# Sliding-window attention with an MLP mixer behind it: half tails on all 128 columns, the last product by blocks of tokens, and another order from the third batch on

## The chip, the cores and the metric

The kernel runs on one core of a Trainium2 chip. The metric is the time of one execution on the device in microseconds (us). An execution is about 280 us long, so 0.2% of it is 0.56 us.

The engines are named as the profile names them: PE is TensorE's matmul, PEld its weight load, DVE is VectorE, ACT is ScalarE, POOL is GpSimd and SP is SyncE, which here only issues DMAs. Results of PE land in PSUM, which has eight banks of 128 partitions by 512 float32.

## The reference

Inputs are q, k, v of 8 batches x 8 heads x 576 tokens x 64, and four weight matrices.

```python
scores = q @ k.T / sqrt(64) - slope[h] * abs(rel)      # rel = query - key
attn   = softmax(where((rel >= 0) & (rel < 128), scores, -1e9))
x      = (attn @ v), heads side by side                # 8 x 576 x 512
h      = relu(x.T @ w_tok1) @ w_tok2                   # mixes tokens, 576 -> 256 -> 576
u      = x + h.T
out    = u + relu(u @ w_ch1) @ w_ch2                   # mixes channels, 512 -> 1536 -> 512
```

## The kernel before, in words

**Tiles.** The batches go in pairs. The 576 tokens of a batch are four blocks of 128 and a tail of 64; the two tails of a pair share one block of 128 rows, the pair's ninth block (`TAIL`). The window is 128, so a block of queries sees its own keys and those of the block before.

**Attention, per block.** `scores` (L646) makes the products of keys by queries on PE (L670): the contraction is 64 long, so these matmuls use half of the array's rows, two heads beside each other. ACT takes the exponential (L693), DVE multiplies by a mask that holds the bias (L703). `values` (L711) multiplies by V with a column of ones beside it (L736): the stationary side is the 128 x 128 block of exponentials, the moving side is 65 columns wide. DVE takes the reciprocal of the sums (L749), and DVE or ACT scales (L752, L758).

**Half tails.** In the first two pairs (`HALVED` is 2, batches 0 to 3) the shared tail block is worked on once for each batch: `half` is 0 or 1, and only that batch's 64 tokens are wanted. There the V matmuls load a stationary side of 64 columns, `a:z`, and write 64 partitions. The plan gives such an operation `mode=2`. In the later pairs the tail is done in one piece.

**Mixers.** `token_mix` (L765) multiplies by w_tok1 (L781, with the tail's matmuls of 64 rows at L791), relu, by w_tok2 (L824, the tail L820), and DVE adds x (L842), which gives u in `ub`. From the third batch on SP turns u by DMA transposes into `uT` (L850). `main` (L993) multiplies by w_ch1 in chunks of 128 hidden rows (L1021, four matmuls of 512 columns a chunk), then relu on ACT or DVE (L1027). `tail_piece` (L1064) does the same for the shared tail once a pair.

**The second product of the channel mixer.** For the 512 tokens outside the tail, `second` (L1135) does it by seven products of half size in place of eight; each is 12 matmuls of 256 columns (L1198), in two groups of six. Sums of the relu's halves (L1046) and of the weights (L568) are made on DVE beforehand. The products are taken in the order 1, 5, 6, 2, 3, 7, 4. They accumulate in three banks, g1, g2 and g3: products 1, 6, 7 and 4 share g2, whose content is evicted after each of them by one DVE add of 128 x 512 (L1169, `evict`) into one of the buffers `ob`. Product 4 may start only when product 7 has been evicted. A finished quarter (256 tokens by 256 channels) is stored by one DMA of 256 KB (L1181). The tail's second product is at L1109, its add at L1116, its store at L1126; in the last batch the tail is cut in two halves of 256 columns, nine matmuls at a time.

**What sets the order.** Nothing is issued as the loops run. Every operation is entered in a `Plan` (L66) with its engine, a cost in ns, a rank, the buffers it makes, reads and uses. `Plan.run` (L118) then lists all engines' work ahead of time: on each engine the operation goes next that can start first by the planner's own clock, ties by rank. PSUM banks come from the ring `ps` by a list of choices: `ONE` is banks 4 to 7, `TWO` the pairs (0,1) and (2,3), which the scores use, `ANY` any single one. The ranks are shifted at random by up to 1500 (`SHIFT`), one seed of `SEEDS` (L337) for each part of the program: part 0 is the attention of the first batch, part b + 1 is `main` of batch b with the attention and token mixing of batch b + 1. `Plan.emit` (L301) writes out the instructions in the order found, so the order on every engine's queue is fixed before the program runs; the hardware only waits for semaphores.

Of the kernel before, what the change touches and what calls it, by code (L numbers as in the profile page):

```python
# [11 lines left out]
ALU = mybir.AluOpType  # L12
# [53 lines left out]
class Plan:  # L66
# [51 lines left out]
    def run(self):  # L118
# [28 lines left out]
        mode, turned = 0, -1e9  # L147
# [53 lines left out]
        def send(o, at, line, work, late):  # L201
            nonlocal flying
            coming.append([at, line, work, o, late])
            flying += 1

        while todo:
            best = None
            for e, c in cand.items():
                pick, early = None, None
                for o in c:  # L210
                    if e == "POOL" and o is not pool[sent]:
                        continue
                    t = max(ready[o], free[e])
# [6 lines left out]
                    for b in o.bufs:  # L220
                        if b.slot is None:
                            got = b.ring.best(b.choice, asked.count(b.choice))
                            asked.append(b.choice)
                            if got is None:
                                t = None
                                break
                            t = max(t, got[0])
# [32 lines left out]
            if e == "PE":  # L260
                slow = 2.0 if t < WARM else 1.0
                if t > free[e] + 1.0:
                    self.gaps.append((free[e], t))
                    if t > free[e] + 3000:
                        slow = 1.6
                    t += 60.0
                elif o.mode != mode:
                    t += 95.0
                mode = o.mode
                o.t0 = t  # L270
                free[e] = t + o.cost * slow
                o.done = free[e] + 165.0
            elif e == "ACT":
                o.t0, free[e], o.done = t, t + o.cost - 115, t + o.cost
            elif e == "DVE":
                o.t0, free[e], o.done = t, t + max(o.cost - 80, 50), t + o.cost
            elif e == "SP":
                o.t0 = t
                if o.bus:
                    free[e] = t + 1310.0  # L280
                    if o.bus > 1500 and len(turns) > 1:
                        free[e] = max(free[e], turns[-2].done + 1100)
                    turns.append(o)
                    send(o, t + 300, 1, TURN[o.bus > 1500][0], TURN[o.bus > 1500][1])
                else:
                    free[e] = t + 590
                    send(o, t + 300, 1, STORE, 1010.0)
            else:
                o.t0 = t
                free[e] = t + o.cost  # L290
                send(o, t + o.cost, 0, STORE if o.packets < 0 else o.packets * PACKET, 1010.0 if o.packets < 0 else LATE[t > FETCH])
                lanes.append(o)
                sent += 1
# [40 lines left out]
RANKH = 0  # L334
RELU = 350
SUMS_AT = 60e3
SEEDS = [45795, 495947, 190309, 331881, 0, 67117, 67408, 179769, 445757]  # L337
SHIFT = 1500.0
UNIT_LATE = False
SECOND_LATE = True  # L340
# [16 lines left out]
STORE = 774.0  # L357
# [11 lines left out]
def kernel(  # L369
# [50 lines left out]
    def bank(choice=ONE):  # L420
        return plan.buf("ps", choice)
# [136 lines left out]
    lt = []  # L558
# [34 lines left out]
    for e in range(2):  # L593
        def go(e=e):
            for i in range(2):
                dve_.tensor_copy(out=maskt[:, e, :, 0, i * R : (i + 1) * R], in_=masks[:, e, :, 0, 0:R])
            dve_.tensor_copy(out=maskt[:, e, :, 1, :], in_=masks[:, e, :, 1, :])
            dve_.memset(maskt[0:R, e, :, 1, R:P], 0.0)
# [112 lines left out]
    def values(pr, blk, half, pb, rank):  # L711
        xb = xbs[pr]
        tail = blk == TAIL
        r0, r1_ = (0, P) if half is None else (half * R, (half + 1) * R)
        vme = held[pr, blk]["v"]
        work = [(r0, r1_, 1, vme)]
        if tail:
            work += [(j * R, (j + 1) * R, 0, held[pr, (j + 1) * NC - 1]["v"]) for j in range(2)
                     if half is None or half == j]
        elif blk % NC:  # L720
            work += [(0, P, 0, held[pr, blk - 1]["v"])]
        both = pr >= PAIRN
        ot = None
        for es in ([[0, 1]] if both else [[0], [1]]):
            n = len(es)
            ot, rt = plan.buf("ps", TWICE) if both else bank(), plan.buf("rt")

            def view(ot=ot, n=n):
                v = ot().rearrange("p (e c) -> p e c", e=n)[:, :, 0 : 4 * (D + 1)]
                return v.rearrange("p e (i d) -> p e i d", i=4)  # L730

            for at, e in enumerate(es):
                def go(e=e, at=at, view=view):
                    mms = [(a, z, kind, vb, i, h) for a, z, kind, vb in work for i, h in enumerate(HEADS[e])]
                    for m, (a, z, kind, vb, i, h) in enumerate(mms):
                        pe_.matmul(view()[a:z, at, i, :], lhsT=pb()[:, e, i, kind, a:z], rhs=vb()[:, h, 0 : D + 1],  # L736
                                   start=m == 0, stop=m == len(mms) - 1, skip_group_check=True)

                rk = rank(240)
                plan.op("PE", 120 * len(work) + (110 if tail and half is None else 0), go, rk,  # L740
                        mode=2 if half is not None else 0, reads=[(pb, e)], uses=[w[3] for w in work],
                        **({"adds": ot} if at else {"makes": ot}))

            def x4(es=es):
                v = xb()[r0:r1_, blk, :].rearrange("p (i e d) -> p e i d", i=4, e=2)
                return v[:, es[0] : es[-1] + 1, :, :]

            def recip(view=view, rt=rt, n=n):
                dve_.reciprocal(out=rt()[r0:r1_, 0:n, :, :], in_=view()[r0:r1_, :, :, D : D + 1])  # L749

            def norm(view=view, rt=rt, n=n, x4=x4):
                dve_.tensor_tensor(out=x4(), in0=view()[r0:r1_, :, :, 0:D],  # L752
                                   in1=rt()[r0:r1_, 0:n, :, :].broadcast_to([r1_ - r0, n, 4, D]), op=ALU.mult)

            def norms(view=view, rt=rt, n=n, x4=x4):
                for e in range(n):
                    for i in range(4):
                        act_.activation(out=x4()[:, e, i, :], in_=view()[r0:r1_, e, i, 0:D], func=ACT.Copy,  # L758
                                        scale=rt()[r0:r1_, e, i, :])

            plan.op("DVE", 180 + 4 * (n - 1), recip, rk, makes=rt, uses=[ot])
            plan.op("DVE", 154 + 270 * n, norm, rk, part=(xb, (blk, half)), uses=[ot, rt],
                    other=("ACT", 115 + 830 * n, norms))
# [370 lines left out]

    def second(b, rank, r2, ss, sums, ub):  # L1135
        pr, half = b // 2, b % 2
        g1, g2, g3 = bank(ANY), bank(ANY), bank(ANY)
        obs = {}
        capt = {}

# [15 lines left out]
        BANK = {1: g2, 6: g2, 7: g2, 4: g2, 2: g1, 5: g3, 3: g3}  # L1156
        AFTER = {6: 1, 7: 6, 4: 7, 3: 5}

        def evict(m, bk, row, col, last):
            key = (row, col)  # L1160
            blks = [half * NC + 2 * row, half * NC + 2 * row + 1]
            cols = slice(col * HN, (col + 1) * HN)
            old = obs.get(key)
            ob = old or obs.setdefault(key, plan.buf("ob"))

            def go():
                v = ob().rearrange("p (c n) -> p c n", c=2)
                src = v if old else ub()[:, blks[0] : blks[0] + 2, cols]
                dve_.tensor_tensor(out=v, in0=bk().rearrange("p (c n) -> p c n", c=2), in1=src, op=ALU.add)  # L1169

            rk = rank(0)
            kw = {"adds": ob} if old else {"makes": ob, "reads": [(ub, x) for x in blks]}
            kw["uses"] = [bk]
            capt[m] = plan.op("DVE", 690, go, rk, **kw)
            if not last:
                return
            late = FROM_P <= b < B - 1
            q_ = nc.gpsimd if late else nc.sync

            def store():  # L1180
                q_.dma_start(out=out[b, row * HS : (row + 1) * HS, cols].rearrange("(c p) n -> p c n", p=P),  # L1181
                             in_=ob().rearrange("p (c n) -> p c n", c=2))

            if late:
                plan.dma(store, 2 * P, -1, uses=ob)
            else:
                plan.op("SP", 550, store, rk, uses=[ob])

        DONE = {1: (0, 0, False), 5: (1, 1, False), 6: (0, 1, False), 7: (1, 1, True), 2: (0, 0, True), 3: (0, 1, True), 4: (1, 0, True)}
        for m in PRODUCTS:  # L1190
            l, w, s, tt = L[m]
            bk = BANK[m]
            for g in range(2):
                def go(m=m, g=g, l=l, w=w, bk=bk):
                    for c in range(2):
                        for t in range(3 * g, 3 * g + 3):
                            first = g == 0 and c == 0 and t == 0 and m not in AFTER
                            pe_.matmul(bk()[:, c * HN : (c + 1) * HN], lhsT=l(t, c), rhs=w(t), start=first,  # L1198
                                       stop=g == 1 and t == HK - 1, skip_group_check=True)

                rd, needs = [], []
# [14 lines left out]
                if SECOND_LATE and g == 0 and m not in AFTER:  # L1216
                    marks["wait"].append(op)
            evict(m, bk, *DONE[m])

    def along(base, length, total):  # L1220
        done = [0.0]
# [68 lines left out]
```

## Time and profile before

| | us |
|---|---|
| median of three runs | 279.53 (279.29 to 279.78) |
| the profiled execution | 280.54 |
| its span, first to last instruction | 278.6 |
| PE busy | 271.4, 2825 matmuls |
| DVE busy | 208.0 |
| ACT busy | 136.0 |
| POOL busy | 116.0 |
| TensorE clock granted, mean | 0.997 of full speed |

The profile comes from one execution, which took 1.0 us more than the median of the runs; 1.94 us of it lie outside the span. Matmuls are pipelined and their ends in the trace are modelled, so the time that a group of matmuls takes is read from its start to the start of the next group. Idle time of an engine that is not the bottleneck costs nothing.

### The profile page before, as it was taken

What the parts mean: (1) busy time and instruction counts of PE and PEld (TensorE: products, weight loads), DVE (VectorE), ACT (ScalarE), POOL (GpSimd) and SP (SyncE); (2) the same over time, 40 slices, a digit from 0 to 9 for tenths busy, and PEclk for the clock granted to TensorE, in tenths of its full rate; (3) what the DMA queues carried; (4) which work ended last, traced back from release to release, by engine and by line L of the source; (5) the groups of instructions that cost most, each with busy time, mean ns of one, the idle gap of its engine ahead of it and who ended that gap; (6) DMA issues with size and microseconds to landing.
All of it is one profiled execution on the core that took longest, in us unless ns stands there. A gap on an engine that the chain in (4) does not pass through costs nothing.

```text
span 278.6 us, 6964 instructions
## 1 busy us (share of the span) xinstructions
PE 271.4 (97%) x2825; PEld 180.0 (65%) x2825; DVE 208.0 (75%) x485; ACT 136.0 (49%) x219; POOL 116.0 (42%) x146
## 2 busy tenths in 40 slices
PE   7999999999999999999999999999999999999994
PEld 3664765675686556585567655486667645689883
DVE  7566689978897559862989479673989549876982
ACT  5561885336960189206961097206870079205610
POOL 8999765940256027900486009700472220013000
PEclk9999999999999999999999999999999999999998
DMA  9999999999899999999999979999499750043014
GB/s 133 155 138 152 182 190 192 155 125 203 141 113 100 172 251 123 123 142 180 182 133 158 205 191 88 148 138 240 69 115 99 197 142 2 2 118 129 0 53 137
DMA packets 167535, 38.43 MB, mean 138 GB/s; under 512 B 155792, under 2 KB 166672, under 8 KB 167504
## 3 DMA queue, kind: packets, MB, share of 16 engines
q0 software_dynamic: 116112, 20.03, 92.8%
q1 hardware_dynamic: 50352, 17.70, 32.9%
q8 instruction: 22, 0.36, 0.6%
q10 hardware_dynamic: 1040, 0.26, 0.4%
q14 instruction: 9, 0.07, 0.1%
HBM read 35.85 MB, written 9.44 MB: 163 GB/s over the span
## 4 chain that ended last, share of the span: by engine, by line
PE 85%; DMA 6%; POOL 3%; DVE 2%; issue 1%; ACT 1%; SPq 0%; POOLq 0%
PE ps L1198 25%; PE ps L1021 25%; PE ps L736 6%; PE ps L670 5%; PE ps L824 5%; PE ps L781 5%; PE ps L1064 4%; PE ps L943 3%; PE ps L1109 3%; POOL qk L515 3%; DMA qk<-in_k_dram 2%; DMA qk<-in_q_dram 2%; DMA uT<-ub 1%; PE ps L630 1%; PE ps L791 1%
## 5 line engine op out<-in xcount | busy, mean ns | idle before, releaser
L1021 PE MATMUL ps<-uT,WC 128*128 128x512 bf16 x328 | 79.3, 379 | 0.8 <-DMA uT<-ub 0.7
L693 ACT ACTIVATE pe<-ps 128x1024 bf16<-128x1024 f32 (+1 forms) x76 | 63.4, 888 | 30.4 <-PE ps L670 30.1
L515 POOL DMA_DIRECT2D v<-in_v_dram x40 | 34.0, 860 | 92.8 <-PE ps L736 89.0
L1027 ACT ACTIVATE r<-ps 128x512 bf16<-128x512 f32 x75 | 44.4, 601 | 41.4 <-PE ps L1021 39.6
L1021 PEld LDWEIGHTS <-WC 128*128 128x128 bf16 x328 | 29.1, 98 | 31.1 <-issue 2.3
L703 DVE TENSOR_TENSOR pe<-pe,mask 128x1024 bf16<-128x1024 bf16 (+1 forms) x64 | 38.1, 608 | 9.0 <-ACT pe L693 8.5
L1198 PEld LDWEIGHTS <-r 128*128 128x128 bf16 x384 | 37.1, 98 | 7.3 <-issue 0.2
L515 POOL DMA_DIRECT2D qk<-in_k_dram x39 | 33.8, 873 | 2.9 <-DMA v<-in_v_dram 1.4
L515 POOL DMA_DIRECT2D qk<-in_q_dram x39 | 33.5, 864 | 2.4 <-DMA WC<-in_moe_w_ch_dram 1.3
L1198 PEld LDWEIGHTS <-s 128*128 128x128 bf16 x288 | 27.5, 98 | 5.9 <-issue 1.3
L752 DVE TENSOR_TENSOR xb<-ps,rt 128x256 bf16<-128x256 f32 (+1 forms) x72 | 29.0, 416 | 0.7
L736 PEld LDWEIGHTS <-pe 128*128 128x128 bf16 (+1 forms) x560 | 22.4, 100 | 9.2 <-DVE pe L703 2.1
L736 PE MATMUL ps<-v,pe 128*128 128x65 bf16 (+1 forms) x560 | 26.5, 194 | 0.1
L1198 PE MATMUL ps<-WC,r 128*128 128x256 bf16 x192 | 25.4, 273 | 0.0
L1198 PE MATMUL ps<-WT,s 128*128 128x256 bf16 x192 | 24.6, 273 | 0.0
L1198 PE MATMUL ps<-WT,r 128*128 128x256 bf16 x192 | 23.9, 273 | 0.0
L1169 DVE TENSOR_TENSOR ob<-ps,ub 128x512 f32<-128x512 f32 x22 | 15.0, 685 | 10.3 <-PE ps L1198 10.1
L842 DVE TENSOR_TENSOR ub<-ps,xb 128x512 bf16<-128x512 f32 x34 | 21.2, 681 | 1.9 <-PE ps L824 1.8
L670 PEld LDWEIGHTS <-qkT 64*128 64x128 bf16 x560 | 14.8, 94 | 11.2 <-issue 9.8
L670 PE MATMUL ps<-qkT 64*128 64x128 bf16 (+1 forms) x304 | 19.4, 216 | 0.0
L749 DVE RECIPROCAL rt<-ps 128x4 f32<-128x4 f32 (+1 forms) x76 | 12.4, 175 | 8.8 <-PE ps L736 8.2
L1069 ACT ACTIVATE r2t<-ps 128x512 bf16<-128x512 f32 x12 | 7.2, 602 | 22.5 <-PE ps L1064 22.5
(95 smaller groups left out, 340.1 us busy)
## 6 DMA issues: line engine op xcount, KB each, us to landing
out_dram<-ob SPq DMA_DIRECT2D x17, 256.0 KB, 2.6
v<-in_v_dram POOLq DMA_DIRECT2D x32, 128.0 KB, 5.3
qk<-in_k_dram POOLq DMA_DIRECT2D x31, 128.0 KB, 5.5
qk<-in_q_dram POOLq DMA_DIRECT2D x31, 128.0 KB, 5.0
WC<-in_moe_w_ch_dram POOLq DMA_DIRECT2D x8, 384.0 KB, 9.1
out_dram<-raw SPq DMA_DIRECT2D x7, 256.0 KB, 2.8
out_dram<-ob POOLq DMA_DIRECT2D x5, 256.0 KB, 3.4
out_dram<-raw POOLq DMA_DIRECT2D x3, 256.0 KB, 2.9
```

The source lines that it names most:

```text
L515: nc.gpsimd.dma_start(out=to()[p0 : p0 + n, :, :], in_=rows(src, b, s0, n))
L670: pe_.matmul(wide(e)[:, i, kind, a:z], lhsT=ts[kb]()[e * D : (e + 1) * D, NHP + i, :], rhs=ts[blk]()[e * D : (e + 1) * D, i, a:z], start=n ...
L693: act_.activation(out=pb()[:, e, :, lo:, c0:c1_], in_=wide(e)[:, :, lo:, c0:c1_], func=ACT.Exp, scale=scale)
L703: dve_.tensor_tensor(out=o, in0=o, in1=heads(mk, es), op=ALU.mult)
L736: pe_.matmul(view()[a:z, at, i, :], lhsT=pb()[:, e, i, kind, a:z], rhs=vb()[:, h, 0 : D + 1], start=m == 0, stop=m == len(mms) - 1, skip_g ...
L752: dve_.tensor_tensor(out=x4(), in0=view()[r0:r1_, :, :, 0:D], in1=rt()[r0:r1_, 0:n, :, :].broadcast_to([r1_ - r0, n, 4, D]), op=ALU.mult)
L781: pe_.matmul(t1[j]()[:, :], lhsT=W1[:, c, j * P : (j + 1) * P], rhs=xb()[:, blk, :], start=c == 0, stop=False)
L842: plan.op("DVE", 690, lambda blk=blk, ht=ht, hs=hs: dve_.tensor_tensor(out=ub()[:, blk, :], in0=ht()[:, hs], in1=xb()[:, blk, :], op=ALU.a ...
L1021: pe_.matmul(ct()[:, :], lhsT=WC1[:, cb, t * P : (t + 1) * P], rhs=uT()[:, cb, :], start=cb == 0, stop=cb == NCB - 1)
L1027: plan.op("ACT", 600, lambda t=t, ct=ct: act_.activation(out=r2()[:, t, :], in_=ct()[:, :], func=ACT.Relu), rk, part=(r2, t), uses=[ct], o ...
L1169: dve_.tensor_tensor(out=v, in0=bk().rearrange("p (c n) -> p c n", c=2), in1=src, op=ALU.add)
L1198: pe_.matmul(bk()[:, c * HN : (c + 1) * HN], lhsT=l(t, c), rhs=w(t), start=first, stop=g == 1 and t == HK - 1, skip_group_check=True)
```

## The change

1. `values`: for half tails the V matmuls load all 128 columns of the exponentials and write all 128 partitions; the readers behind still take the 64 wanted rows. The operation's `mode=2` is dropped.
2. The planner costs an SP store's transfer in proportion to the operation's cost, in place of a fixed value.
3. Three seeds are changed: of part 3 (`main` of batch 2 with the attention of batch 3), part 7 and part 8. Since the planner goes through the whole program, the order differs from about the middle of batch 1 on.
4. `second`, last batch only: g2 is a pair of banks, products 1, 6 and 7 write their two blocks of 128 tokens in separate banks, and the fourth product is done by `last_product`: for each block six matmuls, one DVE add of 128 x 256 and one store of 128 KB, the first on SP's queue and the second on ACT's.

```diff
@@ Plan.run
-                    send(o, t + 300, 1, STORE, 1010.0)
+                    send(o, t + 300, 1, STORE * o.cost / 550, 1010.0)
-SEEDS = [45795, 495947, 190309, 331881, 0, 67117, 67408, 179769, 445757]
+SEEDS = [45795, 495947, 190309, 755034, 0, 67117, 67408, 759722, 858659]
@@ values
-                    mms = [(a, z, kind, vb, i, h) for a, z, kind, vb in work for i, h in enumerate(HEADS[e])]
+                    mms = [(0 if half is not None else a, P if half is not None else z, kind, vb, i, h)
+                           for a, z, kind, vb in work for i, h in enumerate(HEADS[e])]
...
-                        mode=2 if half is not None else 0, reads=[(pb, e)], uses=[w[3] for w in work],
+                        reads=[(pb, e)], uses=[w[3] for w in work],
@@ second
-        g1, g2, g3 = bank(ANY), bank(ANY), bank(ANY)
+        final = b == B - 1
+        g1, g2, g3 = bank(ANY), bank(TWO if final else ANY), bank(ANY)
...
+        def of(bk, c):
+            at = c * (DM if final and bk is g2 else HN)
+            return bk()[:, at : at + HN]
+
+        def both(bk):
+            return bk().rearrange("p (c n) -> p c n", c=2)[:, :, 0:HN]
...
-                dve_.tensor_tensor(out=v, in0=bk().rearrange("p (c n) -> p c n", c=2), in1=src, op=ALU.add)
+                dve_.tensor_tensor(out=v, in0=both(bk), in1=src, op=ALU.add)
...
+            if final and m == 4:
+                last_product(b, rank, r2, ub, g2, of, capt[7])
+                continue
...
-                            first = g == 0 and c == 0 and t == 0 and m not in AFTER
-                            pe_.matmul(bk()[:, c * HN : (c + 1) * HN], lhsT=l(t, c), rhs=w(t), start=first,
+                            first = g == 0 and t == 0 and (c == 0 or final and bk is g2) and m not in AFTER
+                            pe_.matmul(of(bk, c), lhsT=l(t, c), rhs=w(t), start=first,
...
+    def last_product(b, rank, r2, ub, g2, of, before):
+
+        for c in range(2):
+            ob = plan.buf("ob")
+
+            def go(c=c):
+                for t in range(HK):
+                    pe_.matmul(of(g2, c), lhsT=r2()[:, HK + t, HS + c * P : HS + (c + 1) * P], rhs=WT[:, 3, t, :],
+                               start=False, stop=t == HK - 1, skip_group_check=True)
+
+            def add(c=c, ob=ob):
+                dve_.tensor_tensor(out=ob()[:, 0:HN], in0=of(g2, c), in1=ub()[:, NC + 2 + c, 0:HN], op=ALU.add)
+
+            def store(c=c, ob=ob):
+                (nc.sync, nc.scalar)[c].dma_start(out=out[b, HS + c * P : HS + (c + 1) * P, 0:HN], in_=ob()[:, 0:HN])
+
+            rk = rank(656)
+            plan.op("PE", 656, go, rk, adds=g2, reads=[(r2, HK + t) for t in range(HK)], needs=[lt[0][3], lt[1][3], before])
+            plan.op("DVE", 425, add, rk, makes=ob, uses=[g2], reads=[(ub, NC + 2 + c)])
+            plan.op("SP", 275, store, rk, uses=[ob])
```

## The prediction

> **What bounds the kernel now.** I read the page from the top: the span and the busy shares, then the chain that ended last. A row of the page's busy line gives engine, busy us, share, instructions.
>
> ```profile
> span 278.6 us, 6964 instructions
> PE 271.4 (97%) x2825; PEld 180.0 (65%) x2825; DVE 208.0 (75%) x485; ACT 136.0 (49%) x219; POOL 116.0 (42%) x146
> PE 85%; DMA 6%; POOL 3%; DVE 2%; issue 1%; ACT 1%; SPq 0%; POOLq 0%
> ```
>
> TensorE (PE) is busy for 271.4 of 278.6 us and holds 85% of the chain. A time can move only where PE's own work changes, where PE waits, or behind PE's last matmul. The windows show where it waits; their columns are the stretch, its length, PE, PEld, DVE, ACT and POOL busy with counts, the clock, the DMA share and GB/s.
>
> ```profile
> 80.00:100.00 20.00, 19.34 (x170) 12.70 (x169) 13.13 (x28) 5.41 (x13) 5.25 (x6) 1.00 1.51 138
> 100.00:120.00 20.00, 19.98 (x205) 11.56 (x204) 17.15 (x40) 12.75 (x22) 14.13 (x17) 1.00 1.71 159
> ```
>
> From 80 to 100 us 0.66 us are idle, from 100 to 120 almost nothing; the first gap is one wait of L1021 for the transposed uT, in the timeline below. A busy PE may still run below its rate: the records' ends are modelled, so in the timeline I read starts. A row there is start, us from first start to last end, engine, line, tile shape, count.
>
> ```profile
> 109.15 1.02 PE L1021 MATMUL ps<-uT,WC 128*128 128x512 bf16 x4
> 110.01 0.82 PE L1198 MATMUL ps<-WC,r 128*128 128x256 bf16 x6
> 110.74 0.40 PE L736 MATMUL ps<-v,pe 128*128 128x65 bf16 x8
> ```
>
> Four matmuls of 512 columns take 110.01 − 109.15 = 0.86 us, 0.215 each, so one of 256 columns takes 0.108 by its columns, and six 0.65. The L1198 group took 0.73, so 0.08 was a stall in front of L736 that no wait table lists.
>
> **Half tails at full width.** The change removes nothing from the number of matmuls (2825 in either order); it changes the 96 of the narrow form:
>
> ```profile
> L736 PE MATMUL ps<-v,pe 128*64 128x65 bf16 x96 | 4.3, 198 | 0.0
> 78.98 0.69 PE L736 MATMUL ps<-v,pe 128*64 128x65 bf16 x16
> 79.61 0.82 PE L781 MATMUL ps<-xb,W 128*128 128x512 bf16 x3
> 104.91 0.66 PE L736 MATMUL ps<-v,pe 128*128 128x65 bf16 x16
> 105.40 1.25 PE L1021 MATMUL ps<-uT,WC 128*128 128x512 bf16 x5
> ```
>
> Sixteen narrow ones of batch 2 hold PE for 79.61 − 78.98 = 0.63 us, sixteen wide ones for 105.40 − 104.91 = 0.49. The stream is 65 columns in both; the 0.14 are the change of tile shape on the way in or out. In the listed order such changes fall from 116 to 108, the eight all at half tails. Batch 2 gives −0.14, batch 3, whose sixteen stand in one group as well, −0.14.
>
> The Trainium skill, "TensorEngine Tiling (Array Packing)", Theoretical Speedup, speaks against this edit: with a stationary side of at most 64 columns, column tiles may go up to twice as fast. By it sixteen narrow matmuls would take half of the wide ones' 0.49 us, some 0.25, and widening would cost about 0.24 a batch. The trace has 0.63 against 0.49, the other way: a tail's narrow matmuls of one group all use one tile position, so nothing ran beside them. The sum keeps the rows.
>
> Batch 0's tails I count at nothing, since PE then waits for a load; the saving only lengthens that wait. If the load came earlier, 0.14 to 0.28 would show.
>
> ```profile
> 24.67 0.40 PE L630 MATMUL ps<-ident,qk 128*128 128x128 bf16 x4 [0.25 <-DMA qk<-in_k_dram]
> ```
>
> Batch 1's tails stand in the mixed group at 38.59:
>
> ```profile
> 38.59 1.04 PE L736 MATMUL ps<-v,pe 128*128 128x65 bf16 x24
> 39.57 1.90 PE L1021 MATMUL ps<-uT,WC 128*128 128x512 bf16 x8
> 42.52 3.02 PE L1021 MATMUL ps<-uT,WC 128*128 128x512 bf16 x12
> 45.45 0.42 PE L736 MATMUL ps<-v,pe 128*128 128x65 bf16 x8
> 43.60 0.53 DVE L1046 TENSOR_TENSOR r<-r 128x768 bf16<-128x768 bf16 x1
> 44.05 0.75 DVE L752 TENSOR_TENSOR xb<-ps,rt 128x256 bf16<-128x256 f32 x2
> 44.72 1.28 DVE L703 TENSOR_TENSOR pe<-pe,mask 128x1024 bf16<-128x1024 bf16 x2
> ```
>
> The group takes 0.98; 24 wide ones would take 1.5 x 0.49 = 0.74, so PE gains 0.24. Then L736 at 45.45 reads what the first mask at 44.72 writes: PE is through with its twelve at 42.52 + 12 x 0.215 = 45.10 and stands for 0.35. In the new order four of those twelve come behind this L736, so PE arrives at 42.52 + 8 x 0.215 − 0.24 = 44.00. On DVE one sum (44.05 − 43.60 = 0.45), one norm (half of 44.72 − 44.05, 0.34) and a short reciprocal are no longer ahead of the mask, which so moves forward by some 0.8 and frees L736 at about 44.65. The wait becomes 0.6 to 0.7 in place of 0.35: nearly all of the 0.24 is swallowed. The ends are +0.1 and, if the mask came early enough for no wait at all, −0.24 − 0.35 = −0.59. The seven rows leave DVE no gap of more than a tenth, which is near the upper end: I take −0.1.
>
> **The new order, scores moved behind a waiting matmul.** Changed seeds reorder the work from about 43 us on. One move matters most:
>
> ```profile
> 93.80 1.46 PE L1109 MATMUL ps<-WC,r2t 128*128 128x512 bf16 x6
> 95.19 0.40 PE L670 MATMUL ps<-qkT 64*128 64x128 bf16 x8
> 96.25 1.24 PE L1021 MATMUL ps<-uT,WC 128*128 128x512 bf16 x5 [0.66 <-DMA uT<-ub]
> 88.20 5.56 SPq L850 DMA_TRANSPOSE uT<-ub  x4
> 92.07 4.04 DMA uT<-ub
> ```
>
> Before, eight score matmuls (L670, batch 3's first) fill part of the time until the last transposed block lands at 92.07 + 4.04 = 96.11. In the new order they stand behind the first L1021, which waits for that block. From the end of L1109 (93.80 + 6 x 0.215 = 95.09) to where PE is free for L1021 there were 96.25 − 0.66 − 95.09 = 0.50; allowing 0.08 of it for tile changes paid in either place, 0.42 less cover remains, so the wait grows from 0.66 to about 1.1: +0.42. Queued behind that L1021 on PE are only its own three companions, then the scores; the exps of these start later by the same, on an ACT that was busy for 5.41 of 20 us there. The transposes' place among SP's work is unchanged, and the landing follows L824 and its DVE add (L842), so I let it move with PE. If the landing comes earlier by 1.1 the whole wait goes (−0.66); if it comes later by half of that, +1.0. Between these I take the order's own price, as no row gives the landing another reason to move.
>
> **The new order, stalls left out.** The 0.08 at 110.74 and another a little later,
>
> ```profile
> 112.06 0.41 PE L736 MATMUL ps<-v,pe 128*128 128x65 bf16 x8
> 112.49 1.24 PE L781 MATMUL ps<-xb,W 128*128 128x512 bf16 x5
> ```
>
> where eight take 0.43 in place of 0.24 (0.19), come from V products set close behind the matmuls whose bank or mask they need. In the new order other work stands between at both: −0.27; at worst they turn up at another pair of neighbours (0), which is the second rival.
>
> **The last batch by blocks.** One 128x512 add and one 256 KB store become two 128x256 adds and two 128 KB stores, the second on ACT's queue. PE's count is the same. The pair of banks that the second group now takes is one that scores use, and no scores are left in the last batch: nothing. What stands last changes: before it was the fourth product, in the new order it is the second half of the last tail (L1109, nine matmuls), whose result leaves in two stores.
>
> ```profile
> 272.26 1.15 PE L1109 MATMUL ps<-WC,r2t 128*128 128x256 bf16 x9
> 273.25 1.47 PE L1198 MATMUL ps<-WT,r 128*128 128x256 bf16 x12
> 273.45 0.42 DVE L1116 TENSOR_TENSOR raw<-ps,ub 128x256 f32<-128x256 f32 x1 [0.29 <-PE ps L1109]
> 274.76 0.69 DVE L1169 TENSOR_TENSOR ob<-ps,ub 128x512 f32<-128x512 f32 x1 [0.89 <-PE ps L1198]
> 273.94 1.11 SPq L1126 DMA_DIRECT2D out_dram<-raw  x2
> 275.48 0.38 SPq L1181 DMA_DIRECT2D out_dram<-ob  x1
> ```
>
> These two rows give the time from issue to landing of L1181's and then L1126's stores at the end:
>
> ```profile
> DMA to landing us min/median/max: 2.2/2.2/2.2
> DMA to landing us min/median/max: 1.9/2.0/2.0
> ```
>
> Before: PE's end is 273.25 + 12 x 0.108 = 274.55; then 0.21 to the add, 0.69, 0.03 to the issue, 2.17 (2.2) to land: 3.1. After: 0.22 (from 272.26 + 9 x 0.108 = 273.23 to 273.45), 0.42, 0.07 (273.45 + 0.42 to 273.94), then the second store's issue half a us behind the first (two in 1.11), and 2.0: 3.25. That is +0.15. DVE's saving of 0.27 is spent on the second issue. The wait of the fourth product for the seventh's add (0.69 + 0.2) lies under nine L1109 matmuls (0.98) as before.
>
> The Trainium skill, "DMA: Bandwidth & Descriptors", Anatomy of one DMA, gives about 2.0 us plus bytes over 436 KB per us. By it a 64 KB store lands 0.45 us sooner than one of 256 KB, the end would be −0.15 and the sum lower by 0.3. The rows have 2.0 against 2.2 here, so I keep 0.15 to 0.2.
>
> The store on ACT's queue the trace shows only for early loads of 256 KB:
>
> ```profile
> raw<-in_k_dram ACTq DMA_DIRECT2D x1, 256.0 KB, 4.4
> raw<-in_q_dram SPq DMA_DIRECT2D x1, 256.0 KB, 3.8
> ```
>
> Its add is through 0.98 − 0.22 − 0.42 = 0.3 us before PE's end, the second store of the tail is issued 0.22 + 0.42 + 0.07 + 0.5 = 1.2 us after it: 1.5 us of lead. If ACT's queue is 0.6 slower than SP's, as in these rows, it lands first all the same: 0. With the whole 4.4 us it would land 4.4 − 0.3 = 4.1 behind PE's end, +0.85 on the 3.25. I take 0, since at the end no load stands beside it as there did beside the rows' loads. The planner's new store cost issues nothing itself.
>
> **The sum**, against the profiled execution (280.54 us, 278.6 of them span): −0.14 − 0.14 − 0.1 + 0.42 − 0.27 + 0.15 = −0.08, which gives 280.46 beside 280.54. The median of the runs shown is 279.53, 1.0 below the profiled one; carried over, the forecast is **279.4 us** (279.45), no change that can be seen. What a measurement of this kernel can tell from no change is about 0.2%, 0.56 us.
>
> **Rivals.**
> *Faster.* The transposed block lands early enough that no wait stands at the first L1021 (−0.66 in place of +0.42), or batch 1 keeps its 0.24 and loses its 0.35. For it: DVE was busy only 13.13 of 20 us there, and the adds ahead of the transposes may come sooner in the new order. Against: four transposes issue over 5.56 us on SP whatever PE does. The first alone gives 279.45 − 1.08 = 278.4, the second 279.45 − 0.49 = 278.95; a landing that takes half of the wait away gives 278.9. I put this rival at 278.7.
> *Slower.* A bank that L1021 filled is emptied by ACT (L1027) before a V product may take it. In the new order only 0.81 us of PE work stands between at about 108 us, and 0.91 at about 236. The way takes some 0.2 to the relu, 0.60 for it, and 0.06 back: 0.86, if ACT is free.
>
> ```profile
> 107.89 1.94 ACT L693 ACTIVATE pe<-ps 128x1024 bf16<-128x1024 f32 x2
> 109.71 0.60 ACT L1027 ACTIVATE r<-ps 128x512 bf16<-128x512 f32 x1
> ```
>
> Where a pair of exps is ahead of the relu, it waits up to 109.71 − 107.89 = 1.82 longer. It decides from the point at which the scores' results reach ACT before L1021's. Were it to hit one of the two places at half its price, or both at a quarter, that is +0.9, so 280.3. For it: ACT's rows at 107.89 are packed. Against: the span from 100 to 120 has ACT at 12.75 of 20 us, and DVE takes such a relu over where the planner sees ACT full.
> *The change doesn't do what it says.* The tile changes were hidden and the wide tails take 0.63 as well: +0.28, 279.7, inside the band.
>
> **How the numbers follow.** No visible change, 0.43, with its own range 278.97 to 280.09 (the third rival, 0.08 of it, included); faster 0.35; slower 0.22. The range from 278.5 to 280.3 reaches to the middle of both outer cases. Chances: faster 0.35, same 0.43, slower 0.22.
>
> **What would show it.** Wide tails: no 128*64 form in L736's groups, sixteen in 0.49 at batches 2 and 3. Scores moved: PE's wait for uT grows to about 1.1. Stalls: L736 groups of eight taking 0.24 around 110. End: the last row of DVE is L1116, and 3.2 us lie between PE's last matmul and the last landing. I am wrong if uT's wait is gone, if PE's idle between 100 and 260 passes 0.5, or if the ACT-queue store ends the span.

## The result, and the profile after

The changed kernel took 280.98 us in the median of 14 runs (279.87 to 282.47), the kernel before 279.93 in 14 runs beside it (279.07 to 281.19). The ratio is 1.0047 with a 95% interval of 1.0032 to 1.0062: **slower by about half a per cent**, outside the range of the prediction (278.5 to 280.3). A few executions of e3, e5, e6, e9, e10 and e11 took 457 to 1027 us; they count in the medians given below and not in the ratios or highest times, and where the profiled execution was such a one (e6, e9, e11) its trace is not read.

The profiled execution of the changed kernel was one of its quicker ones, 280.33 us. So its page looks no worse than that of before:

```profile
span 278.2 us, 6928 instructions
PE 269.1 (97%) x2789; PEld 180.1 (65%) x2825; DVE 208.6 (75%) x488; ACT 134.7 (48%) x211; POOL 115.8 (42%) x146
```

36 matmul records are missing (2789 of 2825), the weight loads are complete (PEld x2825); times along PE are therefore read from the loads below. Line numbers are a little higher than in before: L1022 is its L1021, L1110 its L1109, L1178 its L1169, L1210 its L1198, L944 its L943; e5, e9 and e13 have one line more. "Load by load" means that the n-th weight load of one trace is set beside the n-th of another with the same order. This span is 0.4 us shorter than that of before, and the median 1.05 us longer. One profile of each kernel was not enough here. The first thing to learn is which of the waits in a profile belong to the kernel and which to that execution, and that takes several profiles of one order of instructions.

The changed kernel's first profile, PE's timeline, at the places of the prediction:

```profile
79.13 0.66 PE L737 MATMUL ps<-v,pe 128*128 128x65 bf16 x16
79.62 0.81 PE L782 MATMUL ps<-xb,W 128*128 128x512 bf16 x2
...
93.80 1.46 PE L1110 MATMUL ps<-WC,r2t 128*128 128x512 bf16 x6
95.39 1.02 PE L1022 MATMUL ps<-uT,WC 128*128 128x512 bf16 x4
96.35 0.40 PE L670 MATMUL ps<-qkT 64*128 64x128 bf16 x8
```

Sixteen wide matmuls of a half tail take 79.62 − 79.13 = 0.49 us. At 95.39 the first chunk starts 95.39 − (93.80 + 6 x 0.215) = 0.30 behind the tail's second product, and the scores stand behind it, as the order said; the wait is 0.3 at most and not 1.1, because the last transpose landed at 95.26 instead of 96.11, with PE at the same point (93.80) in both.

### The profile page after: what moved, and what is told of

It is laid out like the page before. It is cut to its first block, busy times and chain, and to the rows that moved or that the text cites. A ratio compares the mean times of both kernels' runs of the same rounds, so it can differ in the third digit from the quotient of the medians.

```text
span 278.2 us, 6928 instructions
## 1 busy us (share of the span) xinstructions
PE 269.1 (97%) x2789; PEld 180.1 (65%) x2825; DVE 208.6 (75%) x488; ACT 134.7 (48%) x211; POOL 115.8 (42%) x146
## 4 chain that ended last, share of the span: by engine, by line
PE 82%; DMA 8%; POOL 4%; DVE 2%; issue 2%; ACT 1%; DVEq 0%; POOLq 0%; ACTq 0%
PE ps L1210 26%; PE ps L1022 23%; PE ps L737 6%; DMA WC<-in_moe_w_ch_dram 6%; PE ps L670 5%; PE ps L782 4%; PE ps L825 4%; PE ps L1065 4%; PE ps L1110 4%; POOL qk L515 3%; PE ps L944 3%; DMA qk<-in_q_dram 2%; PE ps L792 1%; PE ps L821 1%; DVE pe L703 1%
## 5 line engine op out<-in xcount | busy, mean ns | idle before, releaser
L1022 PE MATMUL ps<-uT,WC 128*128 128x512 bf16 x306 | 77.7, 379 | 1.3
L1022 PEld LDWEIGHTS <-WC 128*128 128x128 bf16 x328 | 29.2, 98 | 30.6 <-issue 1.6
L1210 PEld LDWEIGHTS <-r 128*128 128x128 bf16 x372 | 35.7, 98 | 6.9 <-issue 0.6
L1210 PEld LDWEIGHTS <-s 128*128 128x128 bf16 x288 | 27.7, 98 | 5.5 <-issue 0.9
L753 DVE TENSOR_TENSOR xb<-ps,rt 128x256 bf16<-128x256 f32 (+1 forms) x74 | 29.8, 417 | 0.7
L737 PEld LDWEIGHTS <-pe 128*128 128x128 bf16 (+1 forms) x560 | 21.9, 98 | 9.4 <-DVE pe L703 3.1
L737 PE MATMUL ps<-v,pe 128*128 128x65 bf16 (+1 forms) x560 | 26.1, 194 | 0.6 <-DVE pe L703 0.4
L1210 PE MATMUL ps<-WC,r 128*128 128x256 bf16 x192 | 25.7, 273 | 0.0
L1210 PE MATMUL ps<-WT,s 128*128 128x256 bf16 x192 | 24.6, 273 | 0.0
L1210 PE MATMUL ps<-WT,r 128*128 128x256 bf16 x180 | 22.3, 273 | 0.0
L1178 DVE TENSOR_TENSOR ob<-ps,ub 128x512 f32<-128x512 f32 x20 | 13.6, 685 | 6.2 <-PE ps L1210 5.9
L1178 DVE TENSOR_TENSOR ob<-ps,ob 128x512 f32<-128x512 f32 x15 | 10.3, 690 | 7.9 <-PE ps L1210 7.9
```

The costliest lines, as they stand in the source:

```text
L1022: pe_.matmul(ct()[:, :], lhsT=WC1[:, cb, t * P : (t + 1) * P], rhs=uT()[:, cb, :], start=cb == 0, stop=cb == NCB - 1)
L1178: dve_.tensor_tensor(out=v, in0=both(bk), in1=src, op=ALU.add)
L1210: pe_.matmul(of(bk, c), lhsT=l(t, c), rhs=w(t), start=first, stop=g == 1 and t == HK - 1, skip_group_check=True)
```

## The experiments

All comparisons are with before, run beside on the same chip. "Order" means the order of instructions on an engine; PE's order parts from that of before at 44.0 us, inside batch 1's part.

The expectations speak of theories. O: the loss comes from the new order; E: from the end; T: from the wide tails. From e5 on, U says more closely that in the last batch the work that reads uT stands too close behind the transposes; its rivals are J, that the spread comes from the loads before 40 us, and S, that fixed stalls near 44 and 110 us are the whole loss. The last batch has a part that the text above doesn't describe: for three groups of hidden rows the first product too is done as seven half-size products of four matmuls each (`unit`, L944, the "unit products"). Some read uT, others `tt`, differences that DVE takes from uT beforehand (`halves`, L908) and that are called sums below.

**The changed kernel again (e1).** No edit.

> The changed kernel once more, unchanged, for a second profile. Theory O (the new order): the median lies about 1.0 us above before, and the profile shows where, as PE waits for uT that the first profile did not have: 0.4 to 1.1 us at the first L1022 near 95 us, or a wait near 248 us, where the first profile had the transposes land within 0.2 us of their use. Theory E (the end): PE ends at the same time as in the first profile (274.1) and the last landing is 0.5 to 1.5 us later. Theory T (wide tails): no wait is longer than in before.

280.86 us (279.79 to 282.58), before 279.61; ratio 1.0050 (1.0025 to 1.0074). The profiled execution took 281.91. The table of PE's waits (us, count, longest):

```profile
PE ps L1022 <- DVE rt L750: 1.2, 1, 1.2
PE ps L1287 <- DVE zero L479: 1.0, 1, 1.0
PE ps L944 <- DVE tt L908: 0.8, 1, 0.8
```

Set beside the first profile load by load, this one runs 0.73 later from 37 to 95 us and 0.66 later from there to 248 us (0.61 for two loads at 222), and departs clearly only twice. The first place, the 1.2 near 37 us, is among the first transfers, where profiles of all kernels differ by some tenths to a us. The second is new: L944, the last batch's first unit product that reads `tt`, waits for what DVE takes (L908) from the transposed block uT. PE's end is 1.53 later, of which 0.87 arise there. The last landing follows the last weight load by 3.44, in the first profile by 3.42, so theory E falls here. Theory O fits, at a place that the prediction didn't look at; e9 tests it.

**Wide half tails alone (e2).**

```diff
-  mms = [(a, z, kind, vb, i, h) for a, z, kind, vb in work ...]
+  mms = [(0 if half is not None else a, P if half is not None else z, kind, vb, i, h) for a, z, kind, vb in work ...]
```

> Before with nothing but the half tails at 128 columns; the order of every engine is that of before. Theories O and E: 0.28 us faster than before in the stages of batches 2 and 3, at most 0.5 in all, and the 0.66 us wait for uT at 96 us stays. Theory T: slower than before by 0.3 to 1.0.

279.51 us beside 279.61; ratio 1.0003 (0.9987 to 1.0019). Load by load against before's first profile, PE gains 0.13 at batch 2 and 0.14 at batch 3; of the second gain 0.12 is lost again by 111 us, in waits behind it. The gain of batch 1's tails, 0.26 by 39.56 us, is gone at 42.02, where PE waits for a mask. Theory T falls. The whole is too small for the measurement to show.

**The last product by blocks alone (e3), and with both stores on SP (e8).** e3 is before with `last_product`, the order on PE unchanged; e8 differs from it by

```diff
-  (nc.sync, nc.scalar)[c].dma_start(...)
+  nc.sync.dma_start(...)
```

> Before with nothing but the last batch's fourth product by blocks; the same seeds and the same order on PE, so the product still stands last. Theories O and T: the last add is 0.27 shorter, the last store half as large: 0.2 to 0.4 us faster. Theory E: the store on ACT's queue lands 0.6 to 2.2 us later than SP's did, the kernel is 0.4 to 1.9 us slower.

> Before with the last product by blocks as in the end-only kernel, but both of its stores on SP's queue. If the store on ACT's queue is what lengthens the time outside the span (2.5 us there, 2.0 in before), it comes back to 2.0 and the kernel is level with before or up to 0.3 faster, though the second store issues 0.5 later (span +0.1 to +0.5 over the end-only kernel). If not, the time outside the span stays at 2.5.

e3: 280.02 beside 279.61, ratio 1.0014 (0.9996 to 1.0032). e8: 279.35 beside 279.83, ratio 0.9982 (0.9967 to 0.9997). In e3's profile the last landing comes 2.94 us behind PE's last weight load, in before 3.31, so the span gains what was expected; the store on ACT's queue lands 1.75 us after its issue, earlier than SP's. Theory E's mechanism is not there. But the time outside the span rose from 2.0 to 2.5 in all of e3's runs. In e8 it is 2.1 (2.10 to 2.20), and its span gains 0.1 at the end: what its edit does in the trace sums to about nothing, so the 0.18% by which it is quicker is not explained. The ACT queue alone is not what sets that time: the changed kernel uses it too and has 2.15, and e12 below has 1.75. What sets it stays open.

**The changed kernel without the last product by blocks (e4).** `final = False` in `second`; PE's order stays.

> The changed kernel without the last product by blocks; the order on PE is that of the changed kernel throughout. Theories O and T: within 0.2 us of the changed kernel, so about 1.0 slower than before. Theory E: faster than the changed kernel by 0.5 to 1.5, level with before.

281.35 us (280.25 to 283.45), ratio 1.0067 (1.0039 to 1.0094): not faster. The test is not a clean one: in this order all four tail stores then queue on SP behind the last product's store, and the last landing comes 4.50 us after the last weight load in place of 3.42. It shows that the product by blocks is no loss in the new order, and no more. With e2 and e3, which find no loss of this size in either edit alone, the order is left as the likely cause.

**The units later (e5).** Unit products of the last batch get `after=249000` on the planner's clock, which puts the three tail pieces ahead of them.

> The changed kernel, except that the planner may not start the last batch's unit products (L944) before 249 us on its clock, so that all three tail pieces (L1065) stand ahead of them, as in before. Theory U (the products that read uT stand too close behind its transposes): the wait of L944 near 250 us is gone, the upper group of times (281.9 to 282.6) goes with it, all times lie between 279.5 and 281.1, the median falls by 0.4 to 0.8 below the changed kernel's. Rival J (the spread comes from the loads before 40 us): median and spread as in the changed kernel, 280.9 and 279.8 to 282.6.

280.26 us (278.77 to 281.27) beside 279.83, ratio 1.0005 (0.9985 to 1.0025). The upper times are gone and the median fell by 0.6 to 0.7, but the profile, of an execution of 281.27 us, still has a wait near 252 us, now of L1211. DVE and PE of that profile:

```profile
250.83 0.76 DVE L909 TENSOR_TENSOR tt<-uT 128x512 bf16<-128x512 bf16 x2 [2.07 <-DMA uT<-ub]
251.50 0.69 DVE L1179 TENSOR_TENSOR ob<-ps,ob 128x512 f32<-128x512 f32 x1
...
249.17 1.95 PE L1066 MATMUL ps<-uTt,WC 128*128 128x128 bf16 x32
252.24 1.47 PE L1211 MATMUL ps<-WT,r 128*128 128x256 bf16 x12 [1.12 <-DVE ob L1179]
```

Here one sees the other half of the mechanism. DVE's order is fixed too: the sums `tt` stand ahead of the eviction L1179, wait 2.07 us for uT, and the eviction, whose bank PE wants next, waits behind them. The PE products had been moved, the DVE sums had not.

**Old seeds of parts 7 and 8 (e6, again e11, profile e12).** `SEEDS[7]` and `SEEDS[8]` as in before, all else as changed; the order differs from 225 us on.

> The changed kernel with the old seeds of parts 7 and 8, so the old kind of order from about 210 us on, and the new order before it. Theory U: no upper group of times, median 280.2 to 280.5. Rival J: 280.9 with the same spread. Rival S (the fixed stalls of the new order near 44 and 110 us are all of it): 280.9 with a smaller spread.

> The kernel with the old seeds of parts 7 and 8 once more, for its profile. Theory U: the last transpose of the last batch lands at least 1 us before the first product that reads it, no wait there, 279.4 to 279.8; the stalls of 0.5 near 44 us and 0.4 near 110 us are as in the changed kernel. Rival J: the low median was this call's chip, 280.5 or more now.

> A profile of the kernel with the old seeds of parts 7 and 8. Theory U: no wait of the first product that reads the last batch's uT, which lands over 1 us ahead of it; what is left of the 1.5 us to the changed kernel (0.8 is the unit's wait) lies behind PE's last matmul, where the product by blocks should stand last: 3.9 us from the last weight load to the end of the span in place of 4.3. Rival: it lies between 222 and 248 us, as stalls of PE that the changed kernel has and this one hasn't.

279.52 beside 279.83, ratio 0.9986 (0.9972 to 1.0001); again 279.34 beside 279.55, ratio 0.9992 (0.9975 to 1.0009). In e12's profile (279.05 us), DVE and PE near 250 us:

```profile
251.02 0.69 DVE L1178 TENSOR_TENSOR ob<-ps,ub 128x512 f32<-128x512 f32 x1 [1.51 <-PE ps L1210]
251.63 0.75 DVE L908 TENSOR_TENSOR tt<-uT 128x512 bf16<-128x512 bf16 x2
...
250.82 1.95 PE L1065 MATMUL ps<-uTt,WC 128*128 128x128 bf16 x32
252.60 1.04 PE L944 MATMUL ps<-uT,WC 128*128 128x256 bf16 x8
```

The last transpose landed at 250.71. The sums follow at 251.63 with no idle time ahead of them, the products at 252.60. Nobody waits for uT here. Behind PE, the last landing comes 2.94 us after the last weight load (3.43 in the changed kernel, where the tail's two stores on SP stand last); the time outside the span is 1.75 in place of 2.15. So two seeds take back the wait, 0.5 at the end and 0.4 outside the span.

**The old seed of part 3 (e7).** `SEEDS[3]` as in before. In the order of the instructions this changes the work from 95 to 136 us only, less than the expectation says: the stall near 44 us stays.

> The changed kernel with the old seed of part 3, so another order from about 43 to 120 us only. Theory U: two groups of times stay, since the unit's products are untouched; the fixed stalls go in part, median 280.4 to 280.8. Rival S: median 279.6 or below, one group of times.

281.47 us (279.93 to 283.71), ratio 1.0057 (1.0032 to 1.0083). No gain from undoing that stretch; but this is a third order and not the old one, and its profile has a wait of 0.66 for uT near 125.5 us that no other has. More telling: e6, e11 and e12 keep the order near 44 and 110 us and are level with before: Rival S, that the fixed stalls there are all of the loss, falls.

**The units on old data (e9, profile e13).** All orders stay; the sums and unit products read the transposed block of batch 6, so the kernel leaves out their dependence on the last batch's transposes, and the last batch's output is not that of the reference. The products' half of the edit (the sums' half does the same):

```diff
-  return lambda cb: uT()[:, 2 * k + cb, h * HS : (h + 1) * HS]
+  return lambda cb: uts[b - 1][0]()[:, 2 * k + cb, h * HS : (h + 1) * HS]
```

> The changed kernel with every engine's order kept, but the last batch's unit products (L944) and the sums ahead of them (L908) read the transposed block of the batch before, which landed 30 us earlier, so the last batch's output is left wrong; its own transposes still run. Theory U: the wait near 250 us cannot occur, the upper group of times is gone (none above 281.3), median 280.1 to 280.4, that is 0.5 to 0.9 below the changed kernel. Rival J: 280.9 with times up to 282.5.

> A profile of the changed kernel with the unit's products on old data (the last batch's output is left wrong). Theory U: no wait of L944 near 250 us; from 218 us to the last weight load PE's stalls sum to 0.8 less than in the second profile of the changed kernel.

280.12 us, ratio 1.0017 (1.0002 to 1.0032); none above 281.2. By the two ratios that is 0.8 to 0.9 below the changed kernel. e13 took 280.51 us, with 0.9 of PE's time spent on waiting for an early load of v, so it is compared at this place and not by its whole time. In it the sums run at once, and the products follow without a gap, although uT landed only at 250.89:

```profile
248.78 0.75 DVE L909 TENSOR_TENSOR tt<-uT 128x512 bf16<-128x512 bf16 x2
...
249.28 1.04 PE L945 MATMUL ps<-uT,WC 128*128 128x256 bf16 x8
250.15 0.60 PE L945 MATMUL ps<-tt,WS 128*128 128x256 bf16 x4
```

**The changed kernel a third time (e14).**

> The changed kernel, a third profile. Theory U: at 250 us a wait between 0 and 1 us, and the time of this execution follows it: 280.4 without, 281.9 or more with 0.8.

282.4 us. DVE, POOL's stores and PE:

```profile
251.07 0.76 DVE L908 TENSOR_TENSOR tt<-uT 128x512 bf16<-128x512 bf16 x2 [1.87 <-DMA uT<-ub]
...
248.30 0.74 POOL L1190 DMA_DIRECT2D out_dram<-raw  x1 [23.21 <-DVE raw L1178]
...
249.62 1.04 PE L944 MATMUL ps<-uT,WC 128*128 128x256 bf16 x8
251.88 0.60 PE L944 MATMUL ps<-tt,WS 128*128 128x256 bf16 x4 [1.23 <-DVE tt L908]
```

The group at 249.62 starts before the last block has landed (250.97), so it does not wait for it; the group that reads the sums does. And the time from issue to landing of SP's transposes between 246.4 and 249 us, first of the changed kernel's first profile, then of this one (the largest is that of the last block):

```profile
DMA to landing us min/median/max: 2.3/2.4/2.4
```

```profile
DMA to landing us min/median/max: 2.3/2.4/3.2
```

In the first profile the last block was issued at 246.54 and landed 2.40 later; DVE's sums stood 0.59 for it. Here the transposes ran behind by a further 0.5, the last was issued at 247.76, POOL's store of 256 KB came 0.53 behind it, and it landed after 3.21. PE stood for 1.23 by the table. Against e13, in which this wait cannot occur, PE loses 0.28 at this place in the first profile, 1.15 in the second and 1.55 in the third. The delay starts in the issue of the second of these transposes, which took 1.97 us in the first profile, 2.31 to 2.54 in e1, e13 and e14; why, no run shows.

The traces together bear the collision with POOL's store out. Where the store was issued 0.96 to 1.10 us behind the last transpose, this landed after 2.40 to 2.41 (first profile, e4, e7); 0.66 behind, after 2.94 (e1); 0.53, after 3.21 (e14); 0.43 and 0.45, after 3.36 and 3.33 (e13, e5). In the old order at the end (both profiles of before, e2, e3, e8, e10, e12) the last transpose but one has the store 0.16 behind it and lands after 3.34 to 3.40; the last has none from 1.19 ahead of it to 1.44 behind and lands after 2.34 to 2.36. So transposes that run half a us late also fall into the store's time, which would give the two groups of times. No run moved the store alone: this is a reading of the rows, not an experiment.

**Before a second time (e15).**

> Before, a second profile. The three kernels with its order up to 96 us showed no wait for uT there: the 0.66 of the first profile is not in this one either, PE's last matmul ends 0.7 to 1.3 us earlier, at 273.0 to 273.9.

279.8 us. PE at the place where the first profile had waited 0.66 for uT:

```profile
93.51 1.46 PE L1109 MATMUL ps<-WC,r2t 128*128 128x512 bf16 x6
94.90 0.40 PE L670 MATMUL ps<-qkT 64*128 64x128 bf16 x8
95.38 1.89 PE L1021 MATMUL ps<-uT,WC 128*128 128x512 bf16 x8
```

L1021 starts 1.87 behind L1109's start. Where nothing waits this is 1.72 (e2, e3), in e8, e10 and e7, whose order is the same here, 1.74 to 1.85, and in before's first profile 2.45. So the 0.66 belonged to one execution in seven; the others wait 0.15 or less.

**Both local edits in the old order (e10).** e2's edit and e8's together.

> Before's order with both local edits: wide half tails, and the last product by blocks with both stores on SP. No new order. If the order alone made the change slower, this is faster than before and than the changed kernel: 0.2 for the tails and 0.4 for the end, 279.1 to 279.3 beside 279.7. If the edits get in each other's way, 279.5 or more.

279.68 beside 279.55, ratio 1.0001 (0.9985 to 1.0018). The 0.5 hoped for is not there to be seen. In the trace both edits do what they did alone (0.13 at batch 2; 3.20 from the last load to the last landing, as in e8). By its ratio the fastest of the kernels tried stays e8, and its interval ends at 0.9997.

## Why the prediction was wrong

**What bounds the kernel** held: PE's order and rate set everything, and with the same order two profiles keep their distance load by load to about 0.01 us between 120 and 220 us.

**Wide tails**: as forecast, −0.13 and −0.14. By the Trainium skill's table ("TensorEngine Tiling (Array Packing)", Theoretical Speedup), as the prediction worked it out, e2 would have been slower by 0.24 a batch; its trace is quicker by 0.13 and 0.14.

**Batch 1**: 0.6 to 0.7 of wait forecast at L736 near 44.65; the changed kernel has L737 at 44.65, where PE was free at 42.63 + 8 x 0.215 = 44.35. A part of the wait came one group earlier, of 0.41 on a mask at 42.13. The 0.24 was swallowed, as said, and in e2 in the old order too.

**Scores moved behind a waiting matmul, +0.42**: this step failed. It took a landing from one execution (96.11 us) as the kernel's own. Measured from the start of L1109's group to that of the first chunk that reads uT, the seven traces with before's order here wait 0.15 or less, but for the first profile. Of seven in the new order (L1110's group to L1022's, 1.39 us where nothing waits, in e13 and e14), two show none, four 0.1 to 0.25 and one 0.6 (e5). The landing itself moves: it comes 1.4 to 1.9 us after the first load of L1110's group in the new order, 1.25 to 1.85 in before's, and 2.42 in the first profile alone. To the fifth matmul on uT, with the scores done in both orders, it takes 2.87 on the mean in the new order and 2.75 in the old, so the move costs about 0.1 and never showed the 1.1 forecast.

**Stalls left out, −0.27**: failed. The changed kernel's L737 at 109.79 starts 0.21 late, and the next group near 111.56 loses nothing:

```profile
107.86 1.89 PE L1022 MATMUL ps<-uT,WC 128*128 128x512 bf16 x8
109.79 0.42 PE L737 MATMUL ps<-v,pe 128*128 128x65 bf16 x8
...
107.34 1.94 ACT L693 ACTIVATE pe<-ps 128x1024 bf16<-128x1024 f32 x2
109.16 1.27 ACT L1028 ACTIVATE r<-ps 128x512 bf16<-128x512 f32 x2
```

107.86 + 8 x 0.215 is 109.58. That is the prediction's second rival, the relu behind a pair of exps (the 1.94 at 107.34 in front of the relus at 109.16), at a quarter of the 0.9 it named. So the old stalls (0.08 and 0.19) went and 0.21 came: −0.06 in place of −0.27.

**The end, +0.15**: the way from the last weight load to the last landing is 3.42 in place of 3.31, +0.12; the term was right. The store on ACT's queue cost nothing there. The figure of the Trainium skill that the prediction set beside this term ("DMA: Bandwidth & Descriptors", Anatomy of one DMA) is given there for DMAs issued by GpSimd, and these stores are SP's: at the end of before's first profile 64 KB landed after 1.92 to 2.03 us and 256 KB after 2.17, so the 0.45 worked out from it does not hold here. Time outside the span was no term at all, and its median rose from 2.0 to 2.15.

**What was missing** is the largest, and it is the step that failed. The prediction priced the new order only where before's profile showed a wait or a stall ("One move matters most", then the stalls near 110 us). The last batch's transposes it put at nothing without giving a reason: it did not ask where the new order takes away a distance that no wait marked. Before (e15), then the changed kernel's first profile:

```profile
247.11 2.58 SPq L850 DMA_TRANSPOSE uT<-ub  x2
...
251.11 0.69 DVE L1169 TENSOR_TENSOR ob<-ps,ub 128x512 f32<-128x512 f32 x1 [1.51 <-PE ps L1198]
251.72 0.75 DVE L907 TENSOR_TENSOR tt<-uT 128x512 bf16<-128x512 bf16 x2
...
252.69 1.04 PE L943 MATMUL ps<-uT,WC 128*128 128x256 bf16 x8
253.57 0.60 PE L943 MATMUL ps<-tt,WS 128*128 128x256 bf16 x4
```

```profile
246.54 1.26 SPq L851 DMA_TRANSPOSE uT<-ub  x1
...
249.04 0.76 DVE L908 TENSOR_TENSOR tt<-uT 128x512 bf16<-128x512 bf16 x2 [0.59 <-DMA uT<-ub]
249.72 0.68 DVE L1178 TENSOR_TENSOR ob<-ps,ob 128x512 f32<-128x512 f32 x1
...
248.86 1.04 PE L944 MATMUL ps<-uT,WC 128*128 128x256 bf16 x8
249.85 0.60 PE L944 MATMUL ps<-tt,WS 128*128 128x256 bf16 x4
```

In before, uT of the last batch lands at 250.80, 0.9 us ahead of the sums and 1.9 ahead of the products. The new order brings the transposes about 2 us forward (last issue 246.54 in place of 248.46) and the products about 4 (248.86 in place of 252.69), and on DVE the sums stand ahead of an eviction. uT lands at 248.94, and the sums stand waiting for it. The distance is gone, and every delay of the landing is added: the 0.28, 1.15 and 1.55 above. From the same weight load near 41 us to the last one PE takes 232.0 to 232.3 us in five traces of before's order (e2, e3, e8, e10, e15; 232.9 in the first profile, with its 0.66), 232.3 in e13, and 232.8, 233.6 and 233.9 in the three of the changed kernel. e9 shows that the dependence costs 0.8 to 0.9 in the median. The loss was 1.05 in the first 14 runs and 1.25 beside e1; of the rest, the end and the time outside the span make about 0.12 and 0.15, and what is left is within the intervals. By a sign that the prediction set itself, PE idle for over 0.5 between 100 and 260 us, it was wrong: single waits of 0.83 and 1.23 stand there in two of three profiles.

A slower kernel was given a chance of 0.22, by a stall that did occur, at 0.21 us, but is not what made the kernel slower.

## What to carry to other kernels

When an order written ahead of time changes, list for every DMA landing that the bounding engine reads, directly or through another engine's queue, how long before its use it comes, in both orders; a place where that distance falls towards nothing is where to expect a loss (here nearly all of it), and the old profile shows no wait there. A wait on a DMA in one profile is a draw from a spread: take a second profile before it becomes a term. And in e5 a waiting instruction held up what stood behind it on its engine: moving PE's reader alone didn't remove the wait while DVE's sums, standing 2.07 us for uT, were in front of an eviction that PE needed (1.12 us).

## What the runs showed of the hardware

With the same order, two executions of the changed kernel keep their distance to 0.01 us for more than 100 us (97 to 221 us); most of the spread of this kernel arises at the first loads, after which the same weight load came at 40.5 to 42.1 us, and at single landings. Of the last batch's transposes of 128x512, the last two landed 2.34 to 2.41 us after their issue with no store from POOL issued up to 0.95 us behind them, 2.94 with a store of 256 KB issued 0.66 behind, and 3.2 to 3.4 with one 0.16 to 0.53 behind; the first two transposes of that batch took 3.1 to 4.4 in the new order without any such store, for a reason not found. The time outside the span differed between kernels, and within some hardly varied: 1.70 to 1.82 in e6 and e11, 2.10 to 2.20 in the changed kernel, 2.42 to 2.50 in e3, but 1.71 to 2.16 in before. What sets it was not found.
